# Output projection by seven half products instead of eight, in one listed order with the last group

## The chip, the cores and the metric

One Trainium2 chip, one of its cores. The metric is the device time of one execution in microseconds (us). The core has five engines with instruction streams of their own: PE (TensorE, matrix products), DVE (VectorE), ACT (ScalarE), POOL (GpSimd) and SP (SyncE, which here only issues DMAs). Each takes its own instructions in the order in which the program wrote them, and they wait for each other through semaphores. In this kernel POOL issues the DMAs that add to what lies at their target ("accumulate"), and SP issues all the others, in order too.

## The reference

`x` has S = 2048 tokens of D = 576 numbers. With `xn = layernorm(x)`, the output is the sum of `x`, a sliding-window attention of `xn`, and an S2-MLP block of `xn`:

```python
def _A_ref(x, wqkv, wo):          # 32 heads of 18, window of 8 tokens, 2 apart
    ...
    o = jnp.einsum("bhsw,bhswd->bhsd", attn, vg)
    return (lambda x, *d: x.transpose(*d))(o, 0, 2, 1, 3).reshape(B, S, D) @ wo
def _B_ref(x, w1, w2, w3, w4):
    ...
    x1 = x + hs
    h2 = _gelu(_layernorm(x1, axis=-1) @ w3) @ w4        # 576 -> 4608 -> 576
    return x1 + h2
xn = _layernorm(x, axis=-1)
return x + _A_ref(xn, A_wqkv, A_wo) + _B_ref(xn, B_w1, B_w2, B_w3, B_w4)
```

The change concerns the last product of `_A_ref`, `o @ wo` (2048 x 576 by 576 x 576), and the end of `_gelu(...) @ w3 ... @ w4` that runs ahead of it.

## The kernel before

**Numbers in two parts.** Every large product is made in the matmul's reduced fp32 format from a high and a low part of both operands: hi·hi + hi·lo + lo·hi. ACT writes the high part (a cast), DVE the low part (a subtraction). 576 rows of a contraction are four blocks of 128 and a tail of 64; the tail's two parts are stacked, so that its three terms take two matmuls. `PAIRS` (line 42) lists the resulting 14 matmuls of one product.

**Seven for eight.** The products with `wqkv` and with `w3` (the later part) are already made by halves: both operands are cut in a 2 x 2 grid, and seven products of sums and differences of the quarters (the names A11, S1, B11, T1 and so on) give the four quarters of the result. A half has 288 rows: two blocks of 128 and a tail of 32, whose parts fill 96 rows. `HALVES` (line 50) lists the seven matmuls of one such product, the last one being the tail's.

**The groups.** From line 1634 on, 24 groups `q` run. In each, PE makes seven products with `w3` (steps P1, P2, P6, P5, P7, P4, P3; `product`, 7 matmuls of 512 columns each), and the eight down tiles of the group before (steps D0 to D7; `down`, 12 matmuls of 288 columns each, 128 tokens by 576). `ORDER` fixes the order of the 15 steps; work of the other engines hangs on a step by `at(step, function)`. `z = q - 24` counts back from the end, so z = -1 is the last group. After a down tile's matmuls, the bank is emptied: for ten of the sixteen token tiles (`YD`) ACT copies it to a staging row (`staging`) and POOL accumulates that row into `yd[t]` in memory; for the others ACT copies it back to `Y` (where it was loaded into the bank first, the "seed") or DVE adds it to `Y`. Then `ahead` prepares the next bank; there are two. Rows of `Y` that belong to the tiles in `YD` serve as scratch: `Z1` to `Z4` are rows 13, 15, 5 and 7, and the staging rows rotate by a counter over `EV[0]`.

**The attention's output** `o` lies in memory as `od`. During the groups z = -5 to -2 SP loads it tile by tile (`load_o`, 4 DMAs), DVE transposes it (`o_turn`, line 217 and 218), and SP stores four tiles at a time to `xd` (`put_o`, 4 DMAs of 320 KB). In the last group `wo` is loaded (6 DMAs, 1440 KB) and split (`split_wo`), and `read_xo` reads the first two blocks of 512 tokens back (768 and 512 KB each). The last group's down tiles run after it, with `split_x` of block 0 and half of block 1 between them.

**The output projection** (line 1857 on) takes 16 tiles of 128 tokens. For each, `mm_tok` issues the 14 pairs for both halves of the 576 output columns: 28 matmuls of 128 x 128 by 128 x 288. DVE adds the two banks to the tile's row of `Y` (line 1875) and SP stores the row. The last tile is done half by half (lines 1881 to 1884). The rows of `Y` that were kept in memory are read back by `load_y` (line 1833).

Of the kernel before, what the change touches and what calls it, by code (L numbers as in the profile page):

```python
# [26 lines left out]
C = 2  # L27
# [90 lines left out]

def dram_ap(t, offset, dims):
    return bass.AP(tensor=t.tensor, offset=t.offset + offset, ap=[list(d) for d in dims])  # L120
# [3 lines left out]
def fused_block(ctx, tc, x, wqkv, wo, w1, w2, w3, w4, out):  # L124
# [36 lines left out]
    TS = KV[0:96, 2:3]  # L161
    ST = None
    xd = {}
# [4 lines left out]
    xn = [dram.tile([D, 512], F32, name=f"xn{b}") for b in range(NB)]  # L168
    td = {(sb, k): dram.tile([HF, 512], F32, name=f"td{sb}{k}")
# [41 lines left out]
    def room(p):  # L211
        nonlocal ST
        ST = p.tile([128, 20, 128], F32, name="st")

    def turn(src, t):
        c = slice(32 * t, 32 * t + 32)
        dve.transpose(ST[:, 4:20, c], src[:, :512].rearrange("p (j c) -> p j c", c=32))
        dve.transpose(ST[:, 0:4, c].rearrange("p (a j) c -> p a j c", a=2),
                      src[:, 512:].rearrange("p (j c) -> p j c", c=32)[:, None, :, :]
                      .to_broadcast([128, 2, 2, 32]))  # L220

    def put(key):
        xd[key] = dram.tile([5, 128, 512], F32, name="xd", bufs=4)
        for q in range(4):
            sp.dma_start(dram_ap(xd[key], 128 * q, [[512, 32], [32 * 512, 20], [1, 128]]),
                         ST[32 * q:32 * q + 32])

    def get(key, xt):
        for k in ((0, 3), (3, 5)):
            sp.dma_start(xt[:, 4 + k[0]:4 + k[1], :].bitcast(F32),  # L230
                         xd[key][k[0]:k[1]].rearrange("k p c -> p k c"))

    def split_x(xt, part=None, scr=None):
        raw = xt.bitcast(F32)
        if part in (None, 0, 2):
            r = xt[:, 9, :] if scr is None else scr.bitcast(F32R)
            act.copy(r[64:128], raw[64:128, 4, :])
            act.copy(xt[0:64, 4, :], raw[0:64, 4, :])
            dve.tensor_tensor(xt[64:128, 4, :], raw[64:128, 4, :], r[64:128].bitcast(F32),
                              op=ALU.subtract)  # L240
        for h in {None: (0, 1), 0: (0,), 1: (1,), 2: (), 3: (0,)}[part]:
            hi, lo = slice(2 * h, 2 * h + 2), slice(2 * h + 5, 2 * h + 7)
            act.copy(xt[:, hi, :], raw[:, lo, :])
            dve.tensor_tensor(xt[:, lo, :], raw[:, lo, :], raw[:, hi, :], op=ALU.subtract)
# [22 lines left out]

    def mm_tok(ps, xs, ws, n):
        for i, (a, b) in enumerate(PAIRS):
            for h in range(2):  # L270
                pe.matmul(ps[:, h, :n], xs(a), ws(b, h), start=i == 0, stop=i == len(PAIRS) - 1)  # L271

# [193 lines left out]
    pool.memset(KV[32:64, 2:3], -1.0)  # L466
    for g in range(4):
        pool.memset(sgn[32 * g:32 * g + 16, :], 1.0)
        pool.memset(low[32 * g:32 * g + 16, :], 0.0)
# [475 lines left out]
    def n_flip(t):  # L945
        c = t % 4 * 32
        dve.transpose(ST[:, 0:18, c:c + 32], rz[t].rearrange("p (j c) -> p j c", c=32))

    def n_put(b, q):
        sp.dma_start(dram_ap(xn[b], 128 * q, [[512, 32], [32 * 512, 18], [1, 128]]),  # L950
                     ST[32 * q:32 * q + 32, 0:18])
# [152 lines left out]
    xp = ctx.enter_context(tc.tile_pool(name="xp", bufs=1, side="right", reuse_waits="tile"))  # L1104

    def xp_tile(b):
        return xp.tile([128, 12 - b, 512], F32R, name=f"x1n{b}")

    for b in (2, 3):
        x1n[b] = xp_tile(b)  # L1110
# [126 lines left out]
    def staging():  # L1237
        evc[0] += 1
        if EV[0] == "nt":
            return ntpool.tile([128, D], F32, name=f"ev{evc[0] % 3}")  # L1240
        if EV[0] is None:
            return evp.tile([128, D], F32, name=f"ev{evc[0] % 5}")
        return temp(EV[0][evc[0] % len(EV[0])], D)
# [52 lines left out]
    def down(t, parts):  # L1296
# [6 lines left out]
        for n, (h, w, p) in enumerate(seq):  # L1303
            for k in range(2):
                pe.matmul(ps[:, k, :HF], h[:, col], w[:, p, k * HF:(k + 1) * HF],  # L1305
                          start=n == 0 and not seed, stop=n == len(seq) - 1,
                          skip_group_check=True)
        if t in YD:
# [5 lines left out]
        else:  # L1314
            spent[0] += 0.75
            dve.tensor_tensor(halves(t), ps[:, :, :HF], halves(t), op=ALU.add)  # L1316
        ahead()
# [113 lines left out]
    def place(k):  # L1431
        return opool.tile([128, 5, 512], F32R, name=f"big{k}")


# [11 lines left out]
    for u, (c, b) in enumerate(units):  # L1446
# [88 lines left out]
        if z == -3:  # L1535
            x2, x3 = xp_tile(2), xp_tile(3)
            for sb in range(2):
                area[sb].update(B11=x2[:, 0:5, :], B21=x2[:, 5:10, :], T3=x3[:, 0:5, :])
# [42 lines left out]
    def downs(g):  # L1581
        s0 = 8 * (g // NWP)
        w1, w0 = W4[2 * (NPL + pair(g))], W4[2 * (NPL + pair(g)) + 1]
        for j in range(8):
            if j < 4:
                yield lambda j=j: down(s0 + 4 + j, [(hid[g, "c22"], w1), (hid[g, "c12"], w0)])
            else:
                yield lambda j=j: down(s0 + j - 4, [(hid[g, "c11"], w0), (hid[g, "c21"], w1)])
# [5 lines left out]
    otile, xo = {}, {}  # L1594
    Wo = None
    worw = {}

    def read_xo(b, tile):
        xo[b] = tile
        get(("o", b), tile)  # L1600

    def load_wo(k):
        r = worw[k] = wopool.tile([128, D], F32, name="wr", bufs=5)
        if k < 4:
            sp.dma_start(r, wo[k * 128:(k + 1) * 128, :])
        else:
            dup_tail(r, wo, 0, D)

    def split_wo(k):
        split_w(Wo[:, k, :], Wo[:, 5 + k, :], worw[k])  # L1610
# [8 lines left out]
    def put_o(b):  # L1619
        nonlocal ST  # L1620
        ST = STS[b % 2]
        put(("o", b))

    def o_turn(t):
        nonlocal ST
        ST = STS[t // 4 % 2]
        turn(otile[t], t % 4)
# [6 lines left out]
    for q in range(NQ):  # L1634
# [6 lines left out]
        if z == -1:  # L1641
            evc_pool.__exit__(None, None, None)
            opc.__exit__(None, None, None)
            EV[0] = (9, 11, 10, 2)
            wop = tc.tile_pool(name="wop", bufs=1, reuse_waits="tile")
            wopool = wop.__enter__()
            Wo = wopool.tile([128, 10, D], F32R, name="Wo")
            for k in range(5):
                load_wo(k)
# [88 lines left out]
        else:  # L1738
            at("D3", split_w4, p)
            at("P4", gelu22)  # L1740
            at("D4", low22)
            at("D5", gelu12)
            at("D6", low12)
            for k, it in enumerate(("P4", "D4", "P3", "P3", "D7")):
                at(it, split_wo, k)
        if -5 <= z <= -2:
            for i, (it, nx) in enumerate((("P6", "D1"), ("P7", "D3"), ("P3", "D5"), ("D6", "D7"))):
# [11 lines left out]
        if -4 <= z < -1:  # L1759
            at("P1", put_o, z + 4)  # L1760
        if z == -2:
            at("D7", load_w4, NPL + pair(q + 1), 1)
            at("D7", put_o, 3)

        if z == -1:
            at("P2", lambda: read_xo(0, xp_tile(2)))
            at("P5", lambda: read_xo(1, ring_block(("o", 1))))
        tiles = list(downs(q - 1) if q else plain_downs())
        for it in ORDERS.get(q, ORDER).split():
# [42 lines left out]
            if (z < -6 or z == -6 and EV[0]) and (q, it) != (NWP, "P6"):  # L1812
                bg(1.5 - spent[0], it == "P6" and q != NWP - 1 or (q, it) == (NWP, "P3"))
                spent[0] = 0.0
                if (z, it) == (-6, "P4"):
                    while not state["done"]:
                        bg(1e9)
                    apc.__exit__(None, None, None)
                    opc = tc.tile_pool(name="op", bufs=1, reuse_waits="tile")
                    opool = opc.__enter__()  # L1820
                    STS = [place(k).bitcast(F32).rearrange("p a (b c) -> p (a b) c", c=128)
                           for k in range(2)]
# [5 lines left out]
    h21 = hid[NQ - 1, "c21"] = gelu_ps("c21", ca, Z4)  # L1828
    tiles = list(downs(NQ - 1))

    def load_y(ts):
        for t in ts:
            sp.dma_start(Y[:, t, :], yd[t])

    for j in range(8):
        tiles[j]()
        if j == 0:
            low_part(h21, Z4)
            load_y((1, 2, 5))
            rows = (3, 13, 15, 9, 11)  # L1840
            EV[0] = tuple(rows[(i - evc[0] - 1) % 5] for i in range(5))
        if j in (0, 1, 3):
            split_x(xo[0], {0: 2, 1: 3, 3: 1}[j])
        if j == 6:
            split_x(xo[1], 0)
        if j == 2:
            read_xo(2, xp_tile(3))
        if j == 5:
            load_y((7,))
            read_xo(3, ring_block(("o", 3)))  # L1850
        if j == 7:
            load_y((3,))
    qpdc.__exit__(None, None, None)
    qpcc.__exit__(None, None, None)
    open_ab()

    for t in range(NT):
        b, i = divmod(t, 4)
        yv = Y[:, t, :].rearrange("p (h c) -> p h c", h=2)
        if t == 0:  # L1860
            split_x(xo[1], 1)
        if t in (1, 2):
            split_x(xo[2], t - 1, temp(13))
        if t == 3:
            load_y((9, 10, 11, 13, 15))
        if t in (5, 6):
            split_x(xo[3], t - 5)

        def oT(a, b=b, i=i):
# [44 lines left out]
```

## Time and profile before

| | us |
|---|---|
| median of three runs | 1248.98 |
| lowest and highest | 1247.97 and 1249.2 |
| the profiled execution, whole | 1248.63 |
| its span, first to last instruction | 1246.9 |
| PE busy | 1237.8 |
| DVE busy | 930.1 |
| ACT busy | 759.4 |
| POOL busy | 282.8 |

Lines of the profile read like this. A group of instructions: line of the kernel, engine, operation, written and read tiles, shapes, count, then busy time and mean duration in ns, then the engine's idle time just before it and what ended it. A timeline: start, duration, engine, line, operation, count of merged instructions, and in brackets the idle time before. A wait: who waited, for whom, total us, times, longest. A DMA issue: how many, KB each, median us from issue to landing. SPq and POOLq are the sequencers that issue DMAs. The granted clock is 1.0 throughout, so no PE time is lost to the throttle.

### The profile page before, as it was taken

Reading aid. Unit: us, or ns where it says so; the run is one execution under the profiler, and the core shown is the slowest. Engines: PE = TensorE matmul, PEld = TensorE weight load, DVE = VectorE, ACT = ScalarE, POOL = GpSimd, SP = SyncE. Lnnn points to the kernel's source line nnn. Section 1 sums busy time; section 2 is a strip of 40 time slices with the busy share of each in tenths; the row PEclk is TensorE's granted clock in tenths of the full one; section 3 lists DMA queues with packets and bytes.
Section 4 is the critical chain, followed back from the end, with each engine's and each line's share of the span. In section 5 each row is a group of like instructions: output and inputs, shape, how many; then the busy total and the mean of one; then the engine's idle time right before and its main releaser. Section 6 shows DMA issues by size and latency. Waiting matters only on the chain.

```text
span 1246.9 us, 19980 instructions
## 1 busy us (share of the span) xinstructions
PE 1237.8 (99%) x7361; PEld 1140.0 (91%) x7361; DVE 930.1 (75%) x1182; ACT 759.4 (61%) x1234; POOL 282.8 (23%) x415
## 2 busy tenths in 40 slices
PE   9999999999999999999999999999999999999998
PEld 8999998999899898999899899989899999999998
DVE  8877546698378989997669898889989983554441
ACT  4555566356546555456868667776776776676620
POOL 4523000021321111111223232222232232222200
PEclk9999999999999999999999999999999999999999
DMA  8879796158788876859778988888868779899972
GB/s 234 204 182 222 165 232 188 41 161 242 183 212 200 204 172 125 193 104 240 148 174 170 221 192 182 201 167 209 238 129 178 141 132 197 173 217 230 271 246 77
DMA packets 221130, 230.50 MB, mean 185 GB/s; under 512 B 99544, under 2 KB 158136, under 8 KB 220904
## 3 DMA queue, kind: packets, MB, share of 16 engines
q1 hardware_dynamic: 188280, 162.43, 45.9%
q0 software_dynamic: 32752, 66.80, 33.1%
q8 instruction: 58, 0.95, 0.3%
q14 instruction: 40, 0.33, 0.1%
HBM read 130.76 MB, written 108.82 MB: 192 GB/s over the span
## 4 chain that ended last, share of the span: by engine, by line
PE 66%; DMA 3%; ACT 1%; issue 1%; DVE 1%; SPq 0%; ACTq 0%; POOLq 0%
PE ps L1305 32%; PE cc L1569 20%; PE p L1269 10%; PE ps L271 4%; DMA w3st<-in_B_w_dram 1%; DMA v<-qkvd 1%; DMA xt<-td1T 1%; DMA w3s<-w3st 0%; PE p L1881 0%; ACT Y L1310 0%; ACT Y L1249 0%; DVE Y L1316 0%; DVE w3st L1402 0%; DVE xt L969 0%; SPq L1394 0%
## 5 line engine op out<-in xcount | busy, mean ns | idle before, releaser
L1305 PEld LDWEIGHTS ps<-w,c 128*128 128x128 f32 x3456 | 477.8, 189 | 17.0 <-ACT Y L1310 1.9
L1305 PE MATMUL ps<-w,c 128*128 128x288 f32 x3456 | 487.5, 296 | 1.8 <-ACT Y L1310 0.9
L1311 POOL DMA_DIRECT2D yd<-Y x154 | 138.8, 905 | 366.0 <-ACT Y L1310 306.5
L1260 DVE TENSOR_TENSOR c<-Y,c 128x512 fp32r<-128x512 f32 x144 | 98.8, 687 | 88.2 <-ACT Y L1249 83.4
L1310 ACT COPY Y<-ps 128x576 f32<-128x576 f32 x154 | 97.7, 635 | 74.6 <-PE ps L1305 65.6
L1569 PE MATMUL cc<-xt,w3s 128*128 128x512 f32 (+1 forms) x504 | 127.2, 392 | 0.0
L1569 PEld LDWEIGHTS cc<-xt,w3s 128*128 128x128 f32 (+1 forms) x504 | 92.3, 188 | 17.3
L1313 ACT COPY Y<-ps 128x576 f32<-128x576 f32 x89 | 56.9, 639 | 58.6 <-PE ps L1305 57.1
L1180 DVE TENSOR_TENSOR po<-q,k 128x1152 f32<-128x1152 f32 (+1 forms) x48 | 84.3, 1755 | 2.4 <-DMA k<-qkvd 1.5
L1183 DVE TENSOR_REDUCE L<-po 128x64 f32<-128x1152 f32 (+1 forms) x48 | 84.1, 1751 | 0.8
L1569 PE MATMUL cc<-x1n,w3a 128*128 128x512 f32 (+1 forms) x336 | 84.7, 392 | 0.0
L1248 ACT ACTIVATE c<-p 128x512 fp32r<-128x512 f32 x48 | 28.7, 598 | 89.3 <-PE p L1269 89.2
L1156 DVE TENSOR_TENSOR po<-v,L 128x1152 f32<-128x1152 f32 x56 | 75.4, 1354 | 0.9
L1579 DVE TENSOR_TENSOR Y<-cc,Y 128x512 f32<-128x512 f32 x49 | 33.7, 688 | 52.5 <-ACT Y L1575 46.4
L1569 PEld LDWEIGHTS cc<-x1n,w3a 128*128 128x128 f32 (+1 forms) x336 | 60.4, 188 | 10.0
L453 PE MATMUL p<-wb,xt 128*128 128x432 f32 (+1 forms) x336 | 68.1, 361 | 0.0
L1160 DVE TENSOR_TENSOR po<-po 128x1152 f32<-128x1152 f32 x49 | 66.4, 1355 | 0.9
L453 PEld LDWEIGHTS p<-wb,xt 128*128 128x128 f32 (+1 forms) x336 | 62.5, 188 | 3.1 <-ACT wb L342 0.3
L180 POOL TENSOR_TENSOR rs<-rs,mhalf 128x1 f32<-128x1 f32 x32 | 22.6, 707 | 164.2 <-DVE mv L183 93.3
L1286 ACT COPY ps<-Y 128x576 f32<-128x576 f32 x89 | 57.5, 646 | 3.2 <-DVE Y L1316 1.2
L723 PE MATMUL ca<-wb,xt 128*128 128x432 f32 (+1 forms) x280 | 58.5, 360 | 0.0
L723 PEld LDWEIGHTS ca<-wb,xt 128*128 128x128 f32 (+1 forms) x280 | 52.6, 189 | 2.9 <-ACT keep L730 0.4
(248 smaller groups left out, 2129.8 us busy)
## 6 DMA issues: line engine op xcount, KB each, us to landing
yd<-Y POOLq DMA_DIRECT2D x156, 288.0 KB, 6.3
Y<-in_B_w_dram SPq DMA_DIRECT2D x29, 576.0 KB, 5.6
w3st<-in_B_w_dram SPq DMA_DIRECT2D x56, 256.0 KB, 7.7
qkvd<-stg SPq DMA_DIRECT2D x44, 216.0 KB, 3.3
yd<-ev POOLq DMA_DIRECT2D x26, 288.0 KB, 6.7
w3st<-in_B_w_dram SPq DMA_DIRECT2D x92, 64.0 KB, 7.5
xd<-big SPq DMA_DIRECT2D x16, 320.0 KB, 6.2
Y<-in_A_x_dram SPq DMA_DIRECT2D x16, 288.0 KB, 3.9
```

The costliest lines, as they stand in the source:

```text
L453: pe.matmul(ps[:, :QB], xo[:n, o + k, a, :], W[:n, w + k, v, :], start=i == 0, stop=i == len(PLAIN) - 1)
L723: pe.matmul(ps, form(g // 2, x, n, a), W[:n, OP[w], v, :], start=start and i == 0, stop=stop and i == len(HALVES) - 1, skip_group_check=True)
L1156: dve.tensor_tensor(dst, vv, Lf[:, :, w:w + 1].to_broadcast([128, TPP * GH, HD]), op=ALU.mult)
L1160: dve.tensor_tensor(o, o, dst, op=ALU.add)
L1180: dve.tensor_tensor(dst, qf[:, None, :].to_broadcast([128, n, TPP * GC]), win, op=ALU.mult)
L1183: dve.tensor_reduce(Lw[:, w:w + n, :], dst.rearrange("p w (x d) -> p w x d", d=HD), axis=AX.X, op=ALU.add)
L1260: dve.tensor_tensor(h[:, 1, :], g, h[:, 0, :].bitcast(F32), op=ALU.subtract)
L1269: pe.matmul(ps, W3[f][:, w, :], x1n[b][:, a, :], start=n == 0, stop=n == len(PAIRS) - 1)
L1305: pe.matmul(ps[:, k, :HF], h[:, col], w[:, p, k * HF:(k + 1) * HF], start=n == 0 and not seed, stop=n == len(seq) - 1, skip_group_check=True)
L1310: act.copy(e.rearrange("p (h c) -> p h c", h=2), ps[:, :, :HF])
L1311: pool.dma_start(yd[t], e, accum_op=ALU.add)
L1569: pe.matmul(ps, WX[w][:k, v, SLOT[w], :], area[sb][xk][:k, a, :], start=onto is None and i == 0, stop=last and i == len(HALVES) - 1, skip_ ...
```

## The change

The output projection is made by seven products of halves. A block of 512 tokens is cut in two halves of 256, the 576 contraction rows in two halves of 288 and the output columns likewise. With 128 of the 256 tokens at a time there are eight positions `n` (block `n // 2`), and each takes seven products of seven matmuls with 288 columns: 392 matmuls instead of 448, each with a stationary block of its own.

For it, `wo` is loaded in group z = -5 (6 DMAs: 2 of 576 KB, 4 of 144 KB) rather than in the last. In z = -3 three of its seven forms are cast, in z = -2 DVE makes four sums, and the four other forms are cast in the last group. The transposed `o` goes to `on[b]` (4 DMAs of 288 KB a block), and the four transposes of a block with its store come within one group, at P6, D1, P5 and P4, rather than at P6, P7, P3, D6 and the next P1. A block is read by 2 DMAs of 512 KB and 3 of 128 KB; DVE makes four differences (`sum_x`), ACT the high parts, DVE the low parts, and for the tail ACT writes 96 rows and POOL accumulates 32 of them (`cast_x`, "t"). A product's result goes to a bank (`ca`, `cb`, `cc`); `seed_o` copies `ca` to `cb` on ACT, and `add_o` adds a bank to one half row of `Y`, six times a position.

The last group, its down tiles (D8 to D15; `E` empties a bank, `A` prepares one) and the projection are taken from one list, `ORDER_END`, whose names are called in turn. While the groups z = -5 to -2 run, the staging rotates over three buffers and row 2 rather than over five buffers. Later it rotates over (9, 11, 10, 2), and from the name `rows` on over rows 10, 13, 15, 9 and 11, where before it was 3, 13, 15, 9 and 11.

```diff
+ORDER_END = """
+xlp P1 cb gA lA D0 E0 P6 A0 P2 k2 P7 tf xr0.0 w40 gB wh24 P5 xr0.1 xr0.2 k3 xr0.3 xr0.4 xo1 xo3 D1
+D2 E1 z3 P3 wt04 xr1.0 xr1.1 E2 A1 A2 D3 wh02 g22 lB E3 A3 D4 E4 D5 xh0.01 A4 D6 P4 wl wl02 wl24
+z2 xs0.0 xs0.1 xs0.2 xt0.01 E5 A5 D7 E6 A6 w41 L3 xp1 xt0.13 xh1.01 l22 g12 E7 A7 xr1.2 xl1.01 l12
+D8 xr1.3 xr1.4 E8 D9 xh0.13 gC lC rows xs0.3 E9 xt0.35 L2 xh0.57 xt0.57 A8 D10 E10 A9 D11 E11 L1
+A10 D12 xl0.13 E12 A11 D13 xh1.13 A12 E13 xt1.01 A13 xt1.13 D14 D15 xo2 xh0.35 xr2.0 xr2.1 xr2.2
+xr2.3 xr2.4 E14 E15 A14 xl0.01 xl0.57 A15 out k0.1 c0 k1.1 c1 k0.2 xl0.35 xs1.0 xs1.1 xs1.2 xs1.3
+xh1.35 k0.5 k1.5 y0.2 k2.1 c2 xl1.35 xp2 xt1.35 y0.5 k0.6 y0.6 xl1.13 xh1.57 xl1.57 xh2.01 y1.5
+xt1.57 k1.6 y1.6 k0.3 y0.3 k0.7 y0.7 k1.2 y1.2 k1.3 y1.3 k1.7 y1.7 xt2.13 L7 xt2.01 xl2.01 xh2.13
+k0.4 y0.4 k2.2 k1.4 k3.1 c3 xl2.13 L5 y1.4 xr3.0 xr3.1 xp3 k2.6 y2.2 xs2.0 k2.5 xr3.2 xr3.3 y2.6
+xr3.4 xs2.1 xs2.2 xs2.3 xt2.35 k3.6 y3.6 xh2.35 y2.5 k2.7 y2.7 xt2.57 k3.5 y3.5 xl2.35 k4.1 c4
+k3.7 L10 y3.7 xh2.57 L15 xl2.57 k2.4 y2.4 xt3.13 o4 k4.2 xh3.13 k3.2 y3.2 xt3.01 L9 xs3.0 k4.6
...
+y7.7 o15 k6.4 y6.4 k7.4 y7.4 o12 o13.1
+"""
...
-                at("D3", split_w4, p)
...
+    def load_wo(part):
+        if part == 0:
+            WF["raw"] = wopool.tile([128, 3, 4, HF], F32, name="wr")
+        raw = WF["raw"]
+        if part < 2:
+            k = part
+            sp.dma_start(raw[:, 1:3, 2 * k:2 * k + 2, :].rearrange("p s o c -> p s (o c)"),
+                         wo[HF * k:HF * k + 256, :].rearrange("(s p) c -> p s c", p=128))
...
+    def cast_x(b, what, n0, n1):
...
+            act.activation(d[0:96], src[0:96], AF.Identity, scale=XS)
+            pool.dma_start(d[64:96].bitcast(F32), src[64:96], accum_op=ALU.add)
+            return
...
+            if what == "h":
+                act.copy(hi, src)
+            else:
...
+                dve.tensor_tensor(v[:, :, n0:n1, :], src, hi.bitcast(F32), op=ALU.subtract)
...
-            for i, (it, nx) in enumerate((("P6", "D1"), ("P7", "D3"), ("P3", "D5"), ("D6", "D7"))):
+            for i, (it, nx) in enumerate((("P6", "P6"), ("D1", "D1"), ("P5", "P5"), ("P4", "P4"))):
...
-        if -4 <= z < -1:
-            at("P1", put_o, z + 4)
+        if -5 <= z < -1:
+            at("P4", put_o, z + 5)
...
+        if z == -5:
+            for k, it in enumerate(("D3", "D4", "D5", "D6", "D7", "D7")):
+                at(it, load_wo, k)
+        if z == -3:
+            for it, w, n in (("P2", "h", 0), ("P7", "l", 0), ("P5", "h", 1), ("D3", "l", 1),
+                             ("P1", "t", 0), ("D1", "t", 1)):
+                at(it, cast_wo, 0, w, n, 3 if n else 1, 2 * n)
+        if z == -2:
+            for i, it in enumerate(("D0", "P2", "P7", "P4")):
+                at(it, sum_wo, i)
...
+    def product_o(n, k):
+        b, j = divmod(n, 2)
+        bk, w, x, start, stop = OPROD[k]
+        if start:
+            acc[n, bk] = bank_o(f"{bk}{n % 3}")[:, :HF]
+        ps = acc[n, bk]
+        for i, (a, v) in enumerate(HALVES):
+            pe.matmul(ps, slot_x(b, a, OF[x], slice(128 * j, 128 * j + 128)), slot_w(v, OF[w]),
+                      start=start and i == 0, stop=stop and i == len(HALVES) - 1,
+                      skip_group_check=True)
+
+    def seed_o(n):
+        cb = acc[n, "cb"] = bank_o(f"cb{n % 2}")[:, :HF]
+        act.copy(cb, acc[n, "ca"])
+
+    def add_o(n, k):
...
+        dve.tensor_tensor(y, acc[n, bk], y, op=ALU.add)
...
+    def last_rows():
+        rows = (10, 13, 15, 9, 11)
+        EV[0] = tuple(rows[(i - evc[0] - 1) % 5] for i in range(5))
```

The names in the list, with `b` a block, `n` a position and `i` a tile's number: `P`, `D`, `E`, `A` as above; `xr`, `xs`, `xh`, `xl`, `xt` read, subtract, and cast a block's high part, low part and tail (`xh0.13` is the forms 1 and 2 of block 0); `wh`, `wl`, `wt` the same for `wo`; `k n.p` is product `p` at position `n`, `c` its seed, `y` its addition; `L` reads a row of `Y` back and `o` stores one; `g`, `l`, `k2`, `k3`, `z2`, `z3` belong to the GELU of the last group; `w40` and `w41` split `w4`; `out` opens the projection's banks.

More of the change, by code (lines that the diff above doesn't have):

```diff
@@ L212, in room @@
         nonlocal ST
[L213 to L244, printed above, removed]
+        ST = p.tile([128, 18, 128], F32, name="st")
     def in_order(blk):
@@ new lines, in fused_block, with bank_o @@
+    for i in range(16):
+        end(f"D{i}", lambda i=i: down_mm(*down_of(g + i // 8, i % 8)))
+        end(f"E{i}", lambda i=i: down_out(down_of(g + i // 8, i % 8)[0]))
+        end(f"A{i}", ahead)
+    for n0, n1 in ((0, 2), (2, 4), (0, 4)):
+        for w in "hlt":
+            end(f"w{w}{n0}{n1}", cast_wo, 1, w, n0, n1, n0)
+    end("wl", room_wl)
+    acc, yout = {}, {}
+    pso = psopool = None
+    fresh_o = {}
+    def bank_o(nm):
+        ps = fresh_o.pop(nm, None)
+        return psopool.tile([128, 512], F32, name=nm) if ps is None else ps
```

390 lines of the change are left out of this document (271 added, 119 removed).

## The prediction

> **What bounds the kernel now.** The page's busy times come first, then the list of PE's waits, then the chain of waits over the last 120 us, and at last PE's timeline there.
>
> ```profile
> PE 1237.8 (99%) x7361; PEld 1140.0 (91%) x7361; DVE 930.1 (75%) x1182; ACT 759.4 (61%) x1234; POOL 282.8 (23%) x415
> ...
> PE ps L1305 <- DVE Y L1316: 0.6, 1, 0.6
> ...
> 1174.77 1.11 issue
> 1175.87 0.76 DVE Y L1316
> 1176.63 0.04 issue
> 1176.68 6.66 PE ps L1305 x48
> 1183.34 55.98 PE ps L271 x420
> 1239.32 3.73 PE p L1881 x28
> 1243.05 0.02 issue
> 1243.07 0.46 DVE Y L1883
> ```
>
> PE works 99% of the span, and the chain of the last 60 us is the output projection alone: 420 matmuls of line 271, 28 of line 1881, one DVE addition, the last store. PE waits here only once, for 0.6 us, on an addition of line 1316. So matmuls taken out shorten the kernel one for one, as long as PE's operands come in time.
>
> **What goes.** The projection has 448 matmuls in 55.98 + 3.73 = 59.71 us, 133.3 ns each. The list has 56 products of 7, 392 matmuls. The old pairs use a stationary block twice in a row, the new products never; and one matmul in seven has 96 rows. Both are in the trace already:
>
> ```profile
> 1161.53 1.76 PE L1305 MATMUL ps<-w,c 128*128 128x288 f32 x12
> 1163.13 1.77 PE L1569 MATMUL cc<-xt,w3s 128*128 128x512 f32 x7
> 1164.73 11.35 PE L1305 MATMUL ps<-w,c 128*128 128x288 f32 x84
> 1176.68 6.66 PE L1305 MATMUL ps<-w,c 128*128 128x288 f32 x48 [0.59 <-DVE Y L1316]
> ```
>
> Line 1881 changes its stationary block at every matmul and takes 3.73/28 = 133.2 ns. A product of line 1569 is built like the new ones (seven, the last of 96 rows) and starts 1.60 us before the next step, 229 ns for each of seven with 512 columns; a down tile takes the same 1.60. So 392 x 133.3 = 52.3 us, and **7.46 us go**. The page "TensorE: Matmul & The Clock Gate" of the Trainium skill, section "Back-to-back issue gap", gives 288/2.4 + 2.5 = 122.5 ns for such a matmul; the rows say 133, and by the page the gain would be an estimated 6.9 us.
>
> The wait of 0.59 us stood behind an addition that DVE made late, after a split; in the list the additions E8, E10, E12 stand ahead of the low parts. I count it as gone: **-0.6** (from 0 to -0.6).
>
> **What comes: the staging row.** A step (P or D) lasts 1.60 us.
>
> ```profile
> L1311 POOL DMA_DIRECT2D yd<-Y x154: 854/872/1367, 328.5 to 1185.6; - x154
> L1311 POOL DMA_DIRECT2D yd<-ev x26: 854/880/1571, 323.5 to 1146.8; - x26
> ...
> L1311 POOL DMA_DIRECT2D yd<-Y x10: 854/856/880, 1154.8 to 1185.6; - x10
> ...
> DMA to landing us min/median/max: 4.6/7.5/10.0
> ...
> 1176.12 0.64 ACT L1310 COPY Y<-ps 128x576 f32<-128x576 f32 x1 [1.42 <-PE ps L1305]
> ```
>
> There are 154 + 26 = 180 staged copies, ten of them in the last two lists of down tiles, so the counter stands at 170 before E1. Then E1, E3, E5, E6, E7 take rows 2, 9, 11, 10, 2 of (9, 11, 10, 2), and after `rows` E9 takes row 10, which E6 filled. D6 is the 13th step, over at 13 x 1.6 = 20.8 us after P1; with E5 and a tail's cast ahead of it on ACT, E6 is done near 21.9. Its accumulate lands 7.5 us later in this stretch, at 29.4; E9 then takes 0.64, until 30.0. D11, the 19th step, is due at 28.8 and needs that bank: PE waits **1.2 us** (0 with a landing of 4.6, 3.7 with 10.0). Before, E9 had row 3, which was free. Behind E9 on ACT stand xt0.35, xh0.57, xt0.57 and E11, none due at once.
>
> **Forms and DVE.** Durations: 128x256 0.42, 128x288 0.46, 128x512 0.69, 128x1024 1.23.
>
> ```profile
> 1243.07 0.46 DVE L1883 TENSOR_TENSOR Y<-p,Y 128x288 f32<-128x288 f32 x1 [1.39 <-PE p L1881]
> ...
> 1135.14 0.69 DVE L1579 TENSOR_TENSOR Y<-cc,Y 128x512 f32<-128x512 f32 x1 [5.67 <-ACT Y L1575]
> 1135.75 0.70 DVE L217 STREAM_TRANSPOSE big<-Y 128x512 f32<-128x512 f32 x1
> ...
> L438 DVE TENSOR_TENSOR xt<-xt 128x256 fp32r<-128x256 f32 x15 | 6.1, 417 | 1.4 <-ACT xt L431 1.2
> ...
> L244 DVE TENSOR_TENSOR x1n<-x1n 128x1024 fp32r<-128x1024 f32 x4 | 4.9, 1226 | 4.7 <-ACT x1n L243 4.7
> ```
>
> After the last down tile the list gives DVE 48 additions (22.1 us), the differences of blocks 1 to 3 (4.4 + 5.0 + 4.4) and their low parts (3.7 + 5.0 + 4.4): 49 us against 52.3 of PE. Rows that follow at once start 0.08 us early (0.69 long, the next 0.61 later), so 91 operations take 7 less: 42 us. DVE stays behind PE, with a fifth to spare. Cost 0; without the overlap, and with a wait at each addition, up to 7 (a rival below).
>
> Ahead of D8, the 16th step, due at 24.0: DVE has z2 done at about 18.6, then three differences (2.9 at the closer spacing), w41 (1.3), l22, xl1.01 and l12 (0.6 each), so 24.6. D8's last two matmuls, at 25.3, are the first to need l12. Margin 0.7, cost 0 (0 to 3, if the reads are late).
>
> **DMAs.** The two queues between 1163 and 1180 us:
>
> ```profile
> DMA packets 2373, 4.73 MB, mean 278 GB/s; under 512 B 188, under 2 KB 188, under 8 KB 2370
> ...
> q1 hardware_dynamic: 1646, 3.20, 57.6%
> q0 software_dynamic: 724, 1.50, 48.8%
> ...
> xt<-xd SPq DMA_DIRECT2D x1, 512.0 KB, 15.7
> ...
> 1073.92 1.08 SPq L1391 DMA_DIRECT2D w3st<-in_B_w_dram  x2
> ...
> 1086.97 0.84 ACT L1407 CAST w3a<-w3st 128x768 fp32r<-128x768 f32 x1
> ...
> w3st<-in_B_w_dram SPq DMA_DIRECT2D x2, 256.0 KB, 9.7
> ```
>
> In 17 us, SP's queue moved 3.20 MB in 57.6% (327 GB/s while it held the engines), POOL's accumulates 1.50 MB in 48.8% (181 GB/s). Block 0's reads (1.44 MB) and block 1's first (0.52) are issued from 8.2 on, after P7: 6.0 us, with two accumulates of 0.29 MB (3.3 us) between them, and about 1.7 to land: 19.2. xh1.01 and xl1.01 want them at 22 to 23. In z = -5, `wo` adds 1.77 MB, and the store of block 0 (1.18 MB) moves from the next P1 to P4. The cast of line 1407 follows P7, in z = -4 at 1086.97, in z = -5 15 steps (24.0 us) earlier, and P4 ends two steps after P7, near 1066 there. From then to the end of the `w3` loads SP's queue holds 3.29 MB (store, second part of `wo`, `w4`, `w3`: 10.1 us) beside three accumulates (4.9): done by about 1083, as now (issued from 1074 with 9.7 us to landing). ACT casts that pair at 1086.97, and PE misses ACT only at D5, four steps (6.4 us) after P7, near 1093. Cost 0 (to 2). The store frees SP at P4 instead of holding it at P1, and the three evp rows and row 2 serve five copies per 24 us with landings under 10, so nothing waits there.
>
> **Tails.** Sixteen casts of x tails end in a POOL accumulate, and the last matmul of a product reads it. The nearest row is a like transfer of 64 KB:
>
> ```profile
> L1429 POOL DMA_DIRECT2D w3s<-w3st x23: 772/782/798, 595.4 to 1142.9; - x23
> ...
> DMA to landing us min/median/max: 2.4/2.5/5.0
> ```
>
> Tightest is xt2.57: its cast stands right behind k2.7, and k4.6 needs it six products (5.6 us) later, after two more accumulates have left the same rows. With 2.5 I take **0.3**; with 5.0, 2. The page "SBUF — State Buffer", section "SBUF: two separate sides", warns that DMAs issued from POOL starve for descriptors while DVE runs an operation in a two-port mode. The row's 772 to 798 ns of issue beside a busy DVE show none of that here, so I give it only the chance of the slower rival.
>
> **The end.** k7.4, y7.4, a store of 144 KB, as before:
>
> ```profile
> out_dram<-Y SPq DMA_DIRECT2D x15, 288.0 KB, 2.1
> out_dram<-Y SPq DMA_DIRECT2D x2, 144.0 KB, 1.7
> ...
> 1240.14 0.33 SPq L1876 DMA_DIRECT2D out_dram<-Y  x1
> 1241.71 2.17 SPq L1884 DMA_DIRECT2D out_dram<-Y  x2
> ```
>
> But tiles 15 and 12 (288 KB each) are stored within the 2 us ahead of it, where before the last whole tile went at 1240.14, 3.4 us ahead of the last half (1241.71 + 2.17 - 0.33 = 1243.55): **+0.4** (0 to 1).
>
> **Sum.** -7.46 - 0.6 + 1.2 + 0.3 + 0.4 = -6.2. The profiled execution took 1248.6 (span 1246.9), 0.4 under the median, so **1242.4**. With all bounds low 1240.5; with E9 at 3.7, tails 2, end 1, early loads 2: 1248.6 - 7.5 + 8.7 = 1249.8, unlikely together.
>
> **Rivals.** DVE's part in the projection of now, by windows (duration, then PE, PEld, DVE, ACT, POOL):
>
> ```profile
> 1220.00:1240.00 20.00, 20.00 (x152) 20.00 (x152) 4.44 (x6) 0.00 (x0) 0.00 (x0) 1.00 0.20 75
> ```
>
> - *DVE becomes the bound* of the projection: its 42 to 49 us grow by waits, and additions come late to the banks they must free (k3.7, k4.4, k5.7 stand two products behind their addition). For it: DVE's share rises from 4.44 of 20 us to 42 of 52. Against: the overlap in the rows. Price up to 7: about 1248. Chance 0.10.
> - *Late reads*: the first forms come after 22 us, as reads did in the crowded window (512 KB in 15.7 us, behind `wo`, which has moved). ACT then stands at xh0.01 and DVE at xs0.0, E5 and w41 behind them, D7 and D8 wait 2 to 5: 1245 to 1247. Chance 0.09.
> - *Slower: tails land like the big accumulates.* If the 64 KB accumulates, behind 288 KB ones in POOL's order, take 8 to 9 us instead of 2.5, PE waits at k2.1 (1.9), k2.6 (1.2), k4.6 (5.5), k7.6 (2.7) and at D8, with ACT held behind a tail (2.4): 13.7, so 1248.6 - 8.1 + 13.7 + 0.4 = 1254.6. It passes the old time from about 7 us a landing on. Against it: the row's longest is 5.0. Chance 0.07.
> - *The change does not shorten the matmuls*: chains of seven spaced 150 ns would give 58.8 us, 0.9 saved, 1249 with the added waits. Against: line 1881. Chance 0.03.
>
> **How the numbers follow.** The forecast, 1240.5 to 1244.5, has 0.71. A measurement of this kernel can tell 0.2%, 2.5 us, from no change: faster is below 1246.5. The forecast and most of the late reads: 0.79. Within 0.2%: the DVE rival, the matmul rival and a little of the reads, 0.14. Slower 0.07. The range from 1240.5 to 1248 leaves out the slower rival and part of the two that end near 1249.
>
> **What would show it.** 392 matmuls of 288 columns after the down tiles at 133 ns; a PE wait on ACT's E9 before D11, on an accumulate's landing; no wait at D8; DVE busy 42 to 49 us in the last 53; POOL's small accumulates at 2.5 to 5. Wrong it would be by PE waits of some us inside the projection, or before it in z = -5 and -4.

## The result: 14 us slower, all of it lost ahead of the projection

| | before | after |
|---|---|---|
| median, us | 1248.47 (4 runs) | 1262.92 (4 runs) |
| lowest and highest | 1247.97 and 1249.2 | 1259.1 and 1263.78 |
| the profiled execution, its span | 1248.63, 1246.9 | 1262.52, 1260.7 |
| the projection starts at | 1183.34 | 1204.84 |
| its last DVE addition | 1243.07 | 1257.00 |

The ratio is 1.0109, with a 95% interval from 1.0088 to 1.0131. The forecast was 1242.4, from 1240.5 to 1248.

The profile of the changed kernel, first the busy times, then the end of the chain of waits, then the window of the projection (duration, then PE, PEld, DVE, ACT, POOL, granted clock, DMA share, GB/s):

```profile
PE 1237.5 (98%) x7305; PEld 1137.3 (90%) x7305; DVE 959.4 (76%) x1244; ACT 776.4 (62%) x1264; POOL 298.6 (24%) x436
```

```profile
1254.17 2.81 PE ca L2042 x21
...
1257.00 0.46 DVE Y L2055
```

```profile
1204.60:1257.00 52.40, 52.37 (x394) 52.13 (x393) 43.64 (x91) 19.26 (x34) 9.95 (x13) 1.00 0.73 204
```

The projection is what was forecast: 392 matmuls from 1204.84 to 1256.98, 52.1 us where before there were 59.7, PE never idle, DVE busy 43.6. Only it begins 21.5 us later. PE's waits (who, for whom, total, times, longest) from 1040 us on, and the timeline at the largest of them:

```profile
PE cc L1558 <- DVE Y L1568: 6.0, 2, 5.7
PE ps L1288 <- ACT ev L1297: 5.3, 3, 2.9
PE ps L1288 <- ACT Y L1297: 3.9, 3, 1.6
PE cc L1558 <- DMA w3s<-w3st: 0.5, 1, 0.5
```

```profile
1094.51 7.68 PE L1288 MATMUL ps<-w,c 128*128 128x288 f32 x36 [2.90 <-ACT ev L1297]
...
1176.76 3.36 PE L1558 MATMUL cc<-xt,w3s 128*128 128x512 f32 x7 [5.72 <-DVE Y L1568]
1179.91 6.31 PE L1288 MATMUL ps<-w,c 128*128 128x288 f32 x38
...
1196.59 8.25 PE L1288 MATMUL ps<-w,c 128*128 128x288 f32 x60 [1.03 <-ACT Y L1297]
```

The waits sum to 15.7 us; before there was the one of 0.59. And the matmuls behind the long waits are slow: 36 of 133 ns are 4.8 us, here they take 7.68, 2.9 more; seven of 512 columns take 1.77 elsewhere, here 3.36, 1.6 more; 38 take 6.31 instead of 5.1, 1.2 more. That is 5.7 us more, and 21.4 together with the waits: nearly all of the 21.5. Before, the granted clock was 1.00 throughout; after, it is not:

```profile
1090.00:1100.00 10.00, 7.10 (x31) 6.47 (x30) 6.36 (x10) 7.35 (x12) 2.61 (x4) 0.68 0.74 180
...
1170.00:1180.00 10.00, 4.28 (x16) 3.38 (x16) 1.29 (x2) 7.59 (x10) 1.64 (x2) 0.78 0.96 226
```

What was PE waiting for? The chain of waits names it: each time weights on their way from memory, and at last the accumulate of the staging row. SP's timeline in z = -5 (start, duration, what) shows how it came about:

```profile
1111.96 8.56 DMA w3st<-in_B_w_dram
...
1157.49 14.81 DMA Y<-in_B_w_dram
...
1188.64 7.18 DMA yd<-Y
```

```profile
1068.51 4.66 SPq L935 DMA_DIRECT2D on<-st  x4
1073.22 2.42 SPq L1604 DMA_DIRECT2D wr<-in_A_wo_dram  x1
1075.74 2.29 SPq L906 DMA_DIRECT2D Y<-in_B_w_dram  x1
1078.07 2.12 SPq L1608 DMA_DIRECT2D wr<-in_A_wo_dram  x1
1080.36 1.47 SPq L1382 DMA_DIRECT2D w3st<-in_B_w_dram  x2
1081.87 3.97 SPq L1385 DMA_DIRECT2D w3st<-in_B_w_dram  x4
```

```profile
1092.59 0.83 ACT L1398 CAST w3a<-w3st 128x768 fp32r<-128x768 f32 x1 [6.75 <-DMA w3st<-in_B_w_dram]
```

The store of the transposed `o` (`on<-st`) now stands ahead of the `w4` load (`Y<-in_B_w_dram`) and the six `w3` loads. Before, the order was the other, in SP's timeline at the same place:

```profile
1075.04 2.54 SPq L1394 DMA_DIRECT2D w3st<-in_B_w_dram  x4
1077.68 6.67 SPq L1617 DMA_DIRECT2D Y<-od  x4
1084.39 5.72 SPq L225 DMA_DIRECT2D xd<-big  x4
```

There the six were out at 1077.6, and the store followed at 1084.4. Now they are out at 1085.8, and ACT, with its copies of the down tiles behind the cast of that pair, waits 6.75 us. The copies come late, and PE waits for a bank. The same row of `w4` in both kernels, from 1060 to 1160 us (count, size, median from issue to landing), before and then after:

```profile
Y<-in_B_w_dram SPq DMA_DIRECT2D x4, 576.0 KB, 7.2
```

```profile
Y<-in_B_w_dram SPq DMA_DIRECT2D x4, 576.0 KB, 14.2
```

### The profile page after: what moved, and what is told of

It is laid out like the page before. It is cut to its first block, busy times and chain, and to the rows that moved or that the text cites. A ratio compares the mean times of both kernels' runs of the same rounds, so it can differ in the third digit from the quotient of the medians.

```text
span 1260.7 us, 20054 instructions
## 1 busy us (share of the span) xinstructions
PE 1237.5 (98%) x7305; PEld 1137.3 (90%) x7305; DVE 959.4 (76%) x1244; ACT 776.4 (62%) x1264; POOL 298.6 (24%) x436
## 4 chain that ended last, share of the span: by engine, by line
PE 63%; DMA 5%; ACT 2%; DVE 2%; issue 1%; SPq 0%; ACTq 0%; DVEq 0%
PE ps L1288 31%; PE cc L1558 18%; PE p L1252 10%; DMA w3st<-in_B_w_dram 3%; PE ca L2042 2%; PE cc L2042 1%; DMA Y<-in_B_w_dram 1%; PE cb L2042 1%; DMA yd<-Y 1%; DVE w3st L1393 0%; DMA xt<-xn 0%; DVE xt L954 0%; ACT Y L1297 0%; ACT ev L1297 0%; SPq L1382 0%
## 5 line engine op out<-in xcount | busy, mean ns | idle before, releaser
L1288 PE MATMUL ps<-w,c 128*128 128x288 f32 x3456 | 491.7, 298 | 10.1 <-ACT ev L1297 5.3
L1298 POOL DMA_DIRECT2D yd<-Y x159 | 144.3, 910 | 373.5 <-ACT Y L1297 318.2
L1297 ACT COPY Y<-ps 128x576 f32<-128x576 f32 x159 | 100.9, 635 | 72.0 <-PE ps L1288 59.8
L1300 ACT COPY Y<-ps 128x576 f32<-128x576 f32 x89 | 56.9, 639 | 52.3 <-PE ps L1288 51.0
L1558 PE MATMUL cc<-xB,w3a 128*128 128x512 f32 (+1 forms) x336 | 84.7, 392 | 0.0
L1558 PEld LDWEIGHTS cc<-xB,w3a 128*128 128x128 f32 (+1 forms) x336 | 60.5, 188 | 10.0
```

What stands on the lines that cost most here:

```text
L1297: act.copy(e.rearrange("p (h c) -> p h c", h=2), ps[:, :, :HF])
L1298: pool.dma_start(yd[t], e, accum_op=ALU.add)
L1558: pe.matmul(ps, WX[w][:k, v, SLOT[w], :], area[sb][xk][:k, a, :], start=onto is None and i == 0, stop=last and i == len(HALVES) - 1, skip_ ...
```

## The experiments

Eighteen kernels, in the order in which they ran. Runs 4 and 18 leave out the attention's part of the output. "Before" is the kernel before, run beside them on the same chip.

| run | median | before | ratio, 95% interval |
|---|---|---|---|
| 1 kernel before, store at P4 | 1259.01 | 1248.4 | 1.0086 (1.0071 to 1.0101) |
| 2 the same, one store buffer | 1259.14 | 1248.4 | 1.0085 (1.0067 to 1.0103) |
| 3 after, turns later, store at D7, one buffer | 1270.29 | 1248.4 | 1.0186 (1.0159 to 1.0213) |
| 4 after, no loads of `wo` | 1259.38 | 1248.4 | 1.0097 (1.0077 to 1.0118) |
| 5 kernel before, turns as after, store at D7 | 1247.29 | 1248.37 | 0.9989 (0.998 to 0.9999) |
| 6 after, old steps | 1257.43 | 1248.37 | 1.0065 (1.0049 to 1.0081) |
| 7 run 6, other staging rows | 1257.84 | 1248.37 | 1.0079 (1.005 to 1.0108) |
| 8 run 7, `wo` later | 1259.99 | 1248.37 | 1.0085 (1.0058 to 1.0113) |
| 9 after, two buffers, store at D7 | 1249.14 | 1248.57 | 1.0005 (0.9989 to 1.0021) |
| 10 run 9, other staging rows | 1249.47 | 1248.57 | 1.0005 (0.9992 to 1.0017) |
| 11 run 9, store at P4 | 1263.75 | 1248.57 | 1.0121 (1.0098 to 1.0144) |
| 12 run 10, forms of `wo` in the list | 1247.79 | 1248.53 | 0.9993 (0.9982 to 1.0005) |
| 13 run 12, `wo` spread late | 1247.53 | 1248.53 | 0.9998 (0.9987 to 1.001) |
| 14 run 12, E2 and A1 first | 1247.81 | 1248.27 | 1.0 (0.9991 to 1.0009) |
| 15 run 14, `wo` at three places | 1246.06 | 1248.27 | 0.9984 (0.9975 to 0.9993) |
| 16 run 15, sums early, `wo` at two places | 1249.15 | 1247.42 | 1.0013 (0.9999 to 1.0026) |
| 17 run 15, sums early | 1247.46 | 1247.42 | 0.9998 (0.9989 to 1.0006) |
| 18 after, store at D7 from another tile | 1247.71 | 1248.17 | 0.9998 (0.9986 to 1.001) |

### The first four: is it the order, the buffer or the loads of `wo`?

Three theories. The store's new place on SP's queue (theory 1). One store buffer where there were two: the change took the second one's room for `wo`, so a block's first transpose must wait until the last block's store has landed (theory 2). The 1.7 MB of `wo` in z = -5 (theory 3). Runs 1 and 2 bring the first two into the kernel before:

```diff
-            for i, (it, nx) in enumerate((("P6", "D1"), ("P7", "D3"), ("P3", "D5"), ("D6", "D7"))):
+            for i, (it, nx) in enumerate((("P6", "P6"), ("D1", "D1"), ("P5", "P5"), ("P4", "P4"))):
...
-            at("P1", put_o, z + 4)
+            at("P4", put_o, z + 5)
```

> The kernel before, with only the four transposes of a block moved to P6, D1, P5 and P4 and its store to P4, as in the changed kernel; its two store buffers, five staging buffers and the loads of wo in the last group stay. Theory 1 (order on SP's queue: the store now stands ahead of the w4 and w3 loads of its group): slower by 8 to 20 us, 1256 to 1268, with w3st and w4 landing 4 to 6 us later than before and PE waiting on ACT in z = -4 to -1. Theory 2 (one store buffer in place of two): within 2 us of 1248.5, since both buffers are here. Theory 3 (the 1.7 MB of wo in z = -5): within 2 us of 1248.5, since they are not here.

```diff
-                            for k in range(2)]
+                            for k in range(1)] * 2
```

> As the run with the store at P4, and both blocks of a pair now use one store buffer, so that the first transpose of a block waits until the store of the block before has landed. Theory 1: as that run, within 2 us. Theory 2: at least 6 us slower than that run, 1256 or more, with DVE waiting at the first transpose. Theory 3: within 2 us of 1248.5.

Run 1 lost 10.6 us without a byte of `wo` in these groups and without any other part of the change. Its PE waits and its `w4`:

```profile
PE ps L1305 <- ACT ev L1310: 7.2, 5, 2.4
```

```profile
Y<-in_B_w_dram SPq DMA_DIRECT2D x4, 576.0 KB, 14.0
```

Run 2 lost no more, though DVE now does wait at a block's first transpose (the wait is put down to a later DMA of the same queue):

```profile
DVE big L217 <- DMA w3st<-in_B_w_dram: 33.8, 3, 12.6
```

So with the store at P4 the one buffer costs nothing more. Runs 3 and 4 change the changed kernel:

```diff
-            for i, (it, nx) in enumerate((("P6", "P6"), ("D1", "D1"), ("P5", "P5"), ("P4", "P4"))):
+            for i, (it, nx) in enumerate((("P7", "P7"), ("D4", "D4"), ("P3", "P3"), ("D6", "D6"))):
...
-            at("P4", put_o, z + 5)
+            at("D7", put_o, z + 5)
```

> The changed kernel with the transposes of a block at P7, D4, P3 and D6 and its store at D7, behind the w4 and w3 loads of its group, still one store buffer (12.8 us of steps between the store and the next block's first transpose). Theories 1 and 2: most of the loss goes, 1241 to 1246, w3st landing in under 10 us, no PE wait on ACT before the last list. Theory 3: the loss stays, 1258 or more.

```diff
-                at(it, load_wo, k)
...
+                    pool.memset(WF["raw"], 0.0)
```

> The changed kernel without the loads of wo in z = -5; wo's tile is set to zero by POOL in z = -6 instead, so the output lacks the attention's part. Theory 3: the loss goes, 1241 to 1246. Theory 1 or 2: 1257 to 1262, with the first PE wait on ACT in z = -4 smaller by at most 2 us and those from z = -3 on as in the changed kernel.

Run 3 was slower still. Its time is one that theory 3 allows (1258 or more), but its waits are others. Its DVE and PE in z = -4, and DVE's wait in the two groups after it:

```profile
1099.72 0.78 DVE L1757 STREAM_TRANSPOSE st<-Y 128x576 f32<-128x576 f32 x1 [9.51 <-DMA wr<-in_A_wo_dram]
```

```profile
1106.09 3.25 PE L1288 MATMUL ps<-w,c 128*128 128x288 f32 x12 [7.63 <-ACT ev L1297]
```

```profile
DVE st L1757 <- DMA on<-st: 15.8, 2, 8.5
```

With the store late and one buffer, the next block's first transpose stands still for 9.5 us (put down to a load of `wo` issued behind the store; in the two later groups the profile names the store itself), and behind it, in DVE's order, the work that ACT and PE need. I had counted 12.8 us of steps between store and transpose, but SP, late itself, issued the store only at 1089.1, some 17 us after its step, behind an od read and a load of `wo`. Theory 2 is thus the other half of theory 1: with one buffer, both places of the store that were run have a price. Run 4 gained 3.5 us on the changed kernel, in another batch; the two intervals overlap, so theory 3 is a small part at most.

### The place of the store alone

Run 5 takes run 1 and moves only the store behind the loads:

```diff
-            at("P4", put_o, z + 5)
+            at("D7", put_o, z + 5)
```

> The kernel before with the transposes and the reads of od at P6, D1, P5 and P4, as in the run that cost 10.6 us, but the store at D7, behind the w4 and w3 loads of its group; two store buffers. Theory 1a (the store's place ahead of those loads is what costs): 1247 to 1250.5. Theory 1b (what costs is that transposes and od reads come in the first ten steps of the group, wherever the store stands): 1256 or more.

```profile
1070.86 0.39 SPq L921 DMA_DIRECT2D Y<-in_B_w_dram  x1
1075.36 1.00 SPq L1391 DMA_DIRECT2D w3st<-in_B_w_dram  x2
1076.41 1.98 SPq L1394 DMA_DIRECT2D w3st<-in_B_w_dram  x4
1078.43 4.62 SPq L225 DMA_DIRECT2D xd<-big  x4
```

```profile
Y<-in_B_w_dram SPq DMA_DIRECT2D x4, 576.0 KB, 4.4
```

All of it came back: 11.7 us between two kernels that differ in one step's name (the kernel before took 1248.4 beside both). Theory 1b falls; the transposes and od reads at their new steps cost nothing. `w4` lands in 4.4 us instead of 14.0.

Then the changed kernel. Run 6 gives it the old steps and, for block 1, the tile of `wo`'s forms as a second buffer; runs 7 and 8 vary the staging rows and `wo`:

```diff
+        st = WF["st"] if b == 1 else ST
...
-            at("P4", put_o, z + 5)
+            at("P1", put_o, z + 4)
```

> The changed kernel with the transposes, od reads and stores of blocks 0 to 2 at the steps that they had before (P6, P7, P3, D6, store at the next P1), block 1 in a second buffer that is later the tile of wo's forms, block 3's transposes at P7, D4, P3, D6 and its store at D7; wo's casts start at P7 of z = -3. wo is still loaded in z = -5. Theory 1a: 1241 to 1246 (all of the 20 us gone but for up to 3.5 that the loads of wo cost). Theory 1b: the same. Theory 3 (loads of wo as the main cost) and any cost in the list itself: 1250 or more.

> As the run with the old steps, and the staging rows after `rows` are 13, 15, 10, 9, 11, so that E9 no longer takes the row that E6 filled. If the 1.03 us of PE wait before D11 is that row: 0.7 to 1.3 us faster than that run, and no PE wait before D11. If something else is late there: the same time as that run within 0.4.

> As the run with the other staging rows, and wo's six loads are spread: the first at D7 of z = -5, the second at P6 and the four tails at D7 of z = -4. If the loads of wo crowd the reads of z = -5: 1 to 3 us faster than that run. If 1.7 MB cost the same wherever they stand in these groups: within 1 us of it.

All three stayed slow, at 1257 to 1260. Run 6 has a time that the branch of theory 3 or the list allows (1250 or more), run 7 took 0.4 us more than run 6, and run 8 took 2.2 more than run 7, which neither of its branches has. In run 6, PE has no wait up to 1114, with the store behind the loads, but then ACT and DVE wait three times for the store to land, and PE for them: a cast of `wo` into the second buffer, a transpose of block 3, which shares a buffer with block 2, and a cast of the list into block 3's buffer.

```profile
ACT wfa L1622 <- DMA on<-wfa: 7.7, 1, 7.7
```

```profile
1147.76 0.78 DVE L1760 STREAM_TRANSPOSE st<-Y 128x576 f32<-128x576 f32 x1 [4.84 <-DMA on<-st]
```

In run 9 the two buffers alternate to the end; for that the casts and sums of `wo` move to D6 and D7 of z = -2, and `wh24` a few names later in the list. Run 11 is run 9 with the store back at P4, and nothing else. Of run 9's edit:

```diff
+        st = ST if b % 2 else WF["st"]
...
-            at("P4", put_o, z + 5)
+            at("D5" if z == -2 else "D7", put_o, z + 5)
```

> The changed kernel with its transposes and od reads where it has them (P6, D1, P5, P4), two store buffers that alternate (the second is the tile of wo's forms until z = -2), the store at D7 (D5 in z = -2), behind the w4 and w3 loads, wo's casts and sums at D6 and D7 of z = -2, and wh24 a few steps later in the list. Theory now: of the 20 us lost ahead of the projection all but the staging row's came from the store, by its place ahead of the loads or, in the runs with one buffer, by a transpose or a cast that waits until it has landed. Then 1241 to 1245, PE without a wait from z = -5 to P7 of the last list. If the list itself or the 1.7 MB of wo cost by themselves: 1247 or more, with PE waits in z = -4 and -3 (wo) or in the last list.

> As the run with two buffers throughout, but the store back at P4, ahead of the w4 and w3 loads: the place of the store alone. Theory 1a: 7 to 13 us slower than that run, by PE waits on ACT of 2 to 3 us a group in z = -4, -3, -2 and later. If one buffer was the larger part of the loss: within 4 us of that run.

The pair says the same as runs 1 and 5, by 14.6 us where 7 to 13 were expected. Run 9 itself missed its 1241 to 1245. `w4`, in run 9 and in run 11:

```profile
Y<-in_B_w_dram SPq DMA_DIRECT2D x4, 576.0 KB, 5.0
```

```profile
Y<-in_B_w_dram SPq DMA_DIRECT2D x4, 576.0 KB, 14.4
```

### Why run 9 takes 1249 and not 1242

PE's waits in run 9:

```profile
PE cc L1558 <- DVE Y L1568: 2.8, 1, 2.8
PE ps L1288 <- ACT ps L1269: 1.3, 1, 1.3
PE ps L1288 <- ACT Y L1297: 0.9, 1, 0.9
PE cc L1558 <- ACT cc L1991: 0.5, 1, 0.5
PE ca L2047 <- DMA w3a<-w3a: 0.3, 1, 0.3
```

The 0.9 is the forecast's staging row. Run 10 lets E9 take row 13:

```diff
-        rows = (10, 13, 15, 9, 11)
+        rows = (13, 15, 10, 9, 11)
```

> As the run with two buffers throughout, and the staging rows after `rows` are 13, 15, 10, 9, 11. If the PE wait before D11 is E9's row 10: 0.7 to 1.3 us faster than that run. If something else is late there: within 0.4 of it.

The wait is gone from its profile, so it was the row. The median did not move; the wait behind z3 was 3.6 there and not 2.8, but the runs of each kernel lie 5 to 6 us apart, and why the 0.9 does not show in the time stays open. Runs 12 to 17 went after the others, by moving `wo`'s forms and sums (names in the list) and its loads; run 12 against run 10:

```diff
-... xr0.2 k3 xr0.3 ... D1 D2 E1 wh24 z3 P3 wt04 ...
+... xr0.2 k3 z3 ah1 ah0 al1 al0 xr0.3 ... D1 D2 E1 s0 s1 s2 s3 wh24 P3 wt04 ...
```

> The run with two buffers and the other staging rows, but of wo's forms only the tails are cast at D6 and D7 of z = -2; the high and low parts follow k3 in the list, z3 comes ahead of them, and wo's four sums follow E1, so that neither ACT's seed nor DVE's z3 stands behind a cast or a sum that waits for a tail to land. If the 7 us by which the run with two buffers missed 1242 are these waits (0.5 for the seed, 2.8 and about 1 of lower clock behind z3, 0.9 for the staging row): 1243 to 1245.5, faster than before by 0.3%. If they come from the loads of wo or from the list itself: within 1.5 us of 1249.

> As the run with wo's forms in the list, and wo's loads spread over D7 of z = -4, D7 of z = -3 and D1 of z = -2 instead of z = -5. If the 1.3 us of PE wait in z = -4 comes from wo's 1.7 MB in z = -5: 1 to 2 us faster than that run, with no PE wait on ACT in z = -4. If wo only moves the crowd: the same, with a wait in z = -3 or -2.

> The run with wo's forms in the list, and wh24 and wt04 stand behind E2, A1 and A2 instead of ahead of them. If the 4.18 us by which PE waited for A1's bank in that run are wh24, held on ACT by the sums, in front of E2 and A1: 3 to 4.5 us faster than that run, 1243 to 1245, faster than before. If ACT is short of time in that stretch anyway: the wait moves to a later bank, within 1.5 us of that run.

> As that run, with wo's loads at D7 of z = -5, -4 and -3 (576 KB each). If the 1.35 us of PE wait in z = -4 is wo's 1.7 MB at one place: 1 to 2 us faster than the run with all six in z = -5, with no PE wait ahead of the last list. If any place gives a wait of its own: within 0.7 us.

> As the run with wo's loads at three places, with two edits. In the list, the high parts of wo's forms take w40's place ahead of gB, the sums follow at once, w40 goes behind wh24, and E3 and A3 come ahead of wt04, wh02 and g22. And wo's four tails move from D7 of z = -3 to D7 of z = -5 and -4, so that tile 15's od read is no longer behind them. If the 4.15 us wait for E3's bank is ACT held by wh24 behind the sums, and the 1.13 us in z = -2 that read: both go, 4 to 6 us faster than that run, 1240 to 1242.5, which is the forecast. If ACT or DVE is short of time in the list: the wait moves to a later bank, 1244 or more.

> As that run, with only the edit of the list; wo's tails stay at D7 of z = -3. Expected: 1 to 1.5 us slower than it, with the PE wait of 1.1 us in z = -2 still there, and 3 to 4.5 us faster than the run with wo's loads at three places.

The wait of 1.3 to 1.6 us in z = -4 comes from the loads of `wo` in one place: with them spread (13 and 15) it is gone, and another of 0.8 to 1.1 comes in z = -2, where the last od read stands behind loads of `wo`; with the tails earlier (16) there is one of 1.6 in z = -3. Run 13 gained 0.3 on run 12, run 15 gained 1.75 on run 14. In the list, runs 12, 14 and 15 have one wait of 4.1 to 4.2 us, each time for a bank that ACT fills or empties too late; E2 and A1 first (run 14) only passed it to E3. It is not that ACT had no time there: it stood idle for 4.74 us (run 12) or 2.41 (14 and 15) ahead of `wh24`, a cast that needs DVE's sums, and the copies that empty or fill the bank stand behind that cast. In run 14:

```profile
1162.31 1.16 ACT L1622 CAST wfs<-wr 128x1152 fp32r<-128x1152 f32 x1 [2.41 <-DVE wr L1616]
```

With the sums early the waits there are 0.3 and 2.1 in run 17, 0.8 and 2.1 in run 16 with one of 2.8 behind them, and neither run won anything against the kernel before. Of the kernels with the seven products only run 15 is clear of it: 1246.06, by 0.16% (0.07 to 0.25).

Run 18 needs no room and moves no form: the store, at D7, reads a `w4` tile, so no transpose waits for it.

> The changed kernel with all steps as it has them, wo's loads, forms and staging rows too, but the store at D7 (D5 in z = -2), and it stores a w4 tile of the group in place of the transposed o, so that the output lacks the attention's part and no transpose waits for a store: a second buffer that costs no room. If store order and store buffer are the whole error: 1242 to 1244.5 (the forecast, with up to 1.5 for wo's loads in z = -5 and the row of E9 as forecast), PE waiting only about 1.3 us in z = -4 and 1 us before D11. If the list or the forms of wo cost by themselves: 1246 or more.

```profile
1099.55 1.85 PE L1288 MATMUL ps<-w,c 128*128 128x288 f32 x12 [0.62 <-ACT ps L1269]
1163.19 3.30 PE L1558 MATMUL cc<-xt,w3s 128*128 128x512 f32 x7 [4.12 <-DVE Y L1568]
1181.33 8.25 PE L1288 MATMUL ps<-w,c 128*128 128x288 f32 x60 [0.45 <-ACT Y L1297]
```

```profile
1158.74 1.15 ACT L913 CAST w<-Y 128x1152 fp32r<-128x1152 f32 x1 [7.08 <-DMA on<-w]
```

1247.71 is above what I expected and where the other branch puts it (1246 or more), but the wait of 4.12 us is the experiment's own: the last group's `w4` cast overwrites the tile that the store of block 3 still reads, and ACT, with k3 behind that cast, stood 7.08 us. Without it and the slow matmuls after it (3.30 for 1.77), the profiled execution of 1247.11 would be 1247.11 - 4.12 - 1.53 = 1241.5. That is worked out and was not run, and no run with the whole output came below 1246.06; that the rest of the forecast holds is therefore not shown.

## Why the prediction was wrong

- **Matmuls, -7.46: right.** 59.7 to 52.1 us. The wait behind L1316, -0.6, is gone as said.
- **Staging row, +1.2: right**, 1.03 behind a landing of 7.18, and run 10's profile shows the cause.
- **Tails, +0.3: not seen.** Their accumulates landed in 2.3 to 7.1 us, 4.4 in the median, and not in 2.5, and yet PE waits for none of them in the changed kernel; run 9 has one wait of 0.3. The rival built on them, 1254.6, has the result's sign by luck: its cause did not come.
- **The end, +0.4: not seen.** From the last addition's end to the end of the span it is 1260.7 - 1257.46 = 3.2 us, before 1246.9 - 1243.53 = 3.4.
- **DVE, 42 to 49 us of 52.3: right**, 43.6, and D8 did not wait.
- **The step that failed** is the one on z = -5: "done by about 1083, as now (issued from 1074 with 9.7 us to landing) ... Cost 0 (to 2). The store frees SP at P4 instead of holding it at P1 ... so nothing waits there." That sum does put the store ahead of the loads, but it gives the queue 10.1 us, and POOL's three accumulates 4.9, at the rates of another stretch, and starts as if nothing were still under way. The store was issued at 1068.5 and not near 1066, behind reads of od and the first part of `wo`; the pair of `w3` that ACT needs landed near 1092.5, 24.0 us later and not 17. From 1070 to 1085 us the queues of the changed kernel say:

```profile
DMA packets 3575, 3.58 MB, mean 239 GB/s; under 512 B 210, under 2 KB 2544, under 8 KB 3575
...
q1 hardware_dynamic: 3095, 2.63, 66.2%
q0 software_dynamic: 480, 0.95, 37.9%
```

  SP's queue moved 2.63 MB in 66.2% of 15 us, 265 GB/s while it held the engines, where the sum had 327, from a stretch in which 188 of 2373 packets were under 2 KB. Here it is 2544 of 3575, which fits the pieces of 512 bytes in which the store is written; no run varies the pieces. So the cast that I had at 1086.97 ran at 1092.59, and the margin was smaller too: PE stood from 1091.6 on, not from near 1093, and went on 1.9 us after that cast's start. The cost of 0 (to 2) became waits of 15.7 us and 5.7 of slow matmuls, of which the staging row has 1.03. Runs 1 and 5, and 9 and 11, price the place of the store alone, with the same transfers, at 11.7 and 14.6 us; the rest of the 20.5 by which the forecast missed is not priced one by one.
- Three errors fed it. It was worked out for z = -5 alone, though the store moved in four groups, and SP, late in one, starts the next late. I took "frees SP" for a gain, where the question was who stands behind. And I did not see that one store buffer was left: the change takes out `ST = STS[b % 2]`, and the room went to `wo`. It costs nothing more at P4 (run 2), but it bars the way back to the old order (run 3; in run 6 two blocks share a buffer).
- Of what would show it wrong, the text named "PE waits of some us ... before it in z = -5 and -4". They came there, and it had no rival for them: "late reads" looked only at the reads of the last list.

## What to carry to other kernels

Where the DMA engines are full (here a share of 1.03 and 1.02 in the 20 us from 1070 on), a transfer moved ahead of others on the same in-order queue is paid by those behind it: list them, with the engine that waits for each, in every group in which it happens. Before adding bytes up, take the rate from a stretch with transfers of the same kind, and add what is still under way. When a change needs room, ask which second buffer it took, and which order that forces.

## What the hardware showed unasked

- **The clock.** Behind a long PE wait the matmuls are slow: 2.9 us more after the wait of 2.90, with a granted clock of 0.68 over those 10 us; 2.8 more (1.6 and 1.2) after the wait of 5.72. How long a wait must be for that is no fixed number here: run 17's wait of 2.05 brought 0.83, run 1's of 2.41 nothing:

```profile
1170.00:1180.00 10.00, 9.34 (x49) 8.25 (x50) 8.45 (x14) 7.35 (x13) 4.25 (x5) 0.83 0.83 156
```

```profile
1140.00:1150.00 10.00, 7.59 (x48) 6.57 (x46) 4.32 (x8) 5.34 (x8) 1.71 (x2) 1.00 0.60 139
```

  The page "TensorE: Matmul & The Clock Gate" of the Trainium skill, section "HAM oscillation — how this bites in real kernels", warns of idle gaps of more than about 3.4 us; the section "What's actually happening" calls the window in which activity is counted free-running. By the first, the waits of 2.05 and 2.90 should have cost nothing beyond themselves, and the rows decide. A window that runs on its own would let like waits end differently, as in these two rows; that it is the cause is not shown.

- **Landings by order.** The same load of 576 KB, in the same four groups with 18.8 to 22.2 MB moved from 1060 to 1160 us, landed in 4.4 and 5.0 us (medians of runs 5 and 9) ahead of a store and in 14.0 and 14.4 (runs 1 and 11) behind it. In the kernel before, with the reads of od and the store at other steps, it took 7.2.
